# Windowed attention and a gated feed-forward layer: the second product of the last 3072 tokens as seven block products, stored transposed

## The chip, the cores and the metric

The kernel runs on one core of one Trainium2 chip, in one launch. The metric is the device time of that launch in microseconds. The core has five engines with queues of their own: TensorE (PE in the profile, its weight loads PEld), VectorE (DVE), ScalarE (ACT), GpSimd (POOL, here Pool) and SyncE (SP), which here issues every DMA. Each engine works through its instructions in order and waits on semaphores for the others.

## The reference

Attention over a window (first four heads) or a dilated window (last four), then a feed-forward layer with a gate, all in float32:

```python
scores = scale * np.matmul(q, k.transpose(0, 1, 3, 2))      # 8 batches x 8 heads x 576 tokens x 64
scores = np.where(masks[None, :, :, :], scores, -1000000000.0)
scores = scores - np.max(scores, axis=-1, keepdims=True)
attn = np.exp(scores)
attn = attn / (np.sum(attn, axis=-1, keepdims=True) + 1e-09)
x = np.matmul(attn, v)                                      # as 4608 tokens x 512
...
h = x @ w_in                                                # 512 x 2048
relu6 = np.clip(h + 3.0, 0.0, 6.0)
g = h * relu6 / 6.0
return g @ w_out                                            # 2048 x 512
```

## The kernel before

Every float32 product is made of three matmuls: each operand is split into a high half, rounded to fp32r, and the low half that is left, and high x high, high x low and low x high are added up in PSUM. A high half is a copy with a cast, a low half a subtraction.

The 4608 tokens are twelve chunks of 384 (CH). The first four (PLAIN) go through both products in the plain way: `gemm1` gives 128 features of a chunk, `relu`, `gate`, `gate_high` and `gate_low` make the gated halves, `gemm2` multiplies them with 128 rows of `w_out` into four 128x512 banks of PSUM. The features are 16 steps (NF) of 128.

The last eight chunks, 3072 tokens, are four groups of two chunks. Their **first product** is done in blocks of 2 x 2 (features in two halves, tokens in two halves, the inner dimension in two halves) with seven block products (A11, A12, S2, S1, S3, A22, S4) in place of eight; the sums of weight blocks that this needs are made once (`combo_words`, `combo_sum`, `combo_high`, `combo_low`), written to the DRAM tile `sums`, and read back in each group through a ring of eight SBUF slots (`load_sums`, 512 KB each, two products). The sums of tokens are made in `add_tokens` and split in `fill_high` and `fill_low`. For each of eight pairs of feature steps, `pair` issues the seven products (six matmuls of 384 columns each, L656 to L658) into banks x, y, z of PSUM. Between two products into the same bank ScalarE copies it out (`keep`, L911) and VectorE adds two banks (`add`, L917). Each pair gives four gated tiles of 128x384, which are split at once (L871 high on ScalarE, L875 low on VectorE).

Their **second product** is plain before the change: `unit_part` (L646 to L648) multiplies a gated tile's 128 tokens (as the stationary operand) with 128 rows of `w_out` (512 columns, moving), three matmuls each, into six banks of a group. These units stand on TensorE between the block products of `pair`, and fill the time in which a bank is read. `put_out` scales by 1/6 and writes 128 rows of the output.

Attention is done in 48 blocks of three (head, part) pairs (`block`). The first 12 are in the list ORDER, written by hand. The rest, `attend`, stand at places of the table SPOTS beside the plain chunks, two at once, and then one in each pair. A block's mask is added by VectorE (`add_mask`), then come `largest`, `shifted`, `exponent`; `normalise` divides by the sums.

What sets the order: TensorE's instructions stand in the order of the code. Those of the other engines are put in order by a planner (`_in_time`), from the durations and dependencies that each `op(...)` names; `ahead` says how early an operation may stand before its due time, `takes` and `gives` count slots of the pools `work` (16 tiles) and `wpool` (36) and of PSUM (`ps_h` two banks, `ps_a` six).

Of the kernel before, what the change touches and what calls it, by code (L numbers as in the profile page):

```python
# [39 lines left out]
SPOTS = (30, 1), (33, 1), (36, 1), (39, 1), (42, 1), (45, 1), (52, 1), (56, 1), (59, 1)  # L40
# [34 lines left out]
def windowed_attention_ffn(ctx: ExitStack, tc: tile.TileContext, qk, vp, w, mask, out):  # L75
# [24 lines left out]
    NT, DM = out.shape  # L100
# [147 lines left out]

    def exponent(t):
        return nc.scalar.activation(es[t], es[t], AF.Exp, scale=SCALE)  # L250

# [19 lines left out]
    def block(ts, tv, pools=()):  # L271
# [4 lines left out]
        masked = ts is not None and ts < NFIRST  # L276
# [222 lines left out]
    def gate_high(n):  # L499
        ghs[n] = work_tile("gh", F32R)  # L500
        return nc.scalar.copy(ghs[n], ts[n])
# [49 lines left out]
    STREAMED = (A11, A12, A22, S2, S4, S3, S1)  # L551
    GROUPS = (NCH - PLAIN) // 2
    STREAM = NF // 2 * PRODUCTS // 2
    sums = tc.dram_tile([2 * STREAM, P, 2, HALF], F32, name="sums")
    combos = {}

    def combo_words(k, i):

        if k not in combos:
            combos[k] = w_tile("v", [4, HALF])  # L560
        x, v = win[2 * k + i], combos[k]
        nc.vector.tensor_tensor(
            out=v[:, 2 * i : 2 * i + 2].rearrange("p a n -> p (a n)"), in0=x[:, 0].bitcast(F32), in1=x[:, 1].bitcast(F32), op=ALU.add
        )

    def combo_sum(k, i):

        v = combos[k]
        to, a, b, op = ((3, 2, 3, ALU.add), (2, 0, 2, ALU.subtract), (0, 3, 0, ALU.subtract), (1, 1, 0, ALU.subtract))[i]
        nc.vector.tensor_tensor(out=v[:, to], in0=v[:, a], in1=v[:, b], op=op)  # L570

    def combo_high(k):
        hi = w_tile("sh", [4, HALF], F32R)
        nc.scalar.copy(hi, combos[k])
        combos[k] = combos[k], hi

    def combo_low(k):
        v, hi = combos[k]
        nc.vector.tensor_tensor(out=v.bitcast(F32R), in0=v, in1=hi.bitcast(F32), op=ALU.subtract)

    def streamed(k, i):
        return PRODUCTS * k + STREAMED.index(i)

    def combo_plain(k):
        for i, x, at in ((A11, win[2 * k], 0), (A12, win[2 * k], HALF), (A22, win[2 * k + 1], HALF)):
            nc.sync.dma_start(out=sums[streamed(k, i)], in_=x[:, :, at : at + HALF].bitcast(F32))

    def combo_out(k):
        v, hi = combos.pop(k)
        at = streamed(k, S2)  # L590
        to = sums[at : at + 4].rearrange("n p a x -> p n a x")
        nc.sync.dma_start(out=to[:, :, 0], in_=hi.bitcast(F32))
        nc.sync.dma_start(out=to[:, :, 1], in_=v)
# [3 lines left out]
    def load_sums(at):  # L597
        ring[at] = w_tile("ring", [2, 2, HALF], F32R)
        i = 2 * (at % STREAM)
        nc.sync.dma_start(out=ring[at].bitcast(F32).rearrange("p n a x -> p n (a x)"), in_=sums[i : i + 2].rearrange("n p a x -> p n (a x)"))  # L600
# [35 lines left out]
    banks, begun, ended = {}, set(), {}  # L636

    def unit_part(g, f, at, gh, gl):
        if (g, at) not in banks:
            banks[g, at] = ps_a.tile([P, DM], F32, name="ps_o", tag="ps_a")  # L640
        bank, first = banks[g, at], (g, at) not in begun
        begun.add((g, at))
        ended[g, at] = ended.get((g, at), 0) + 1
        final = ended[g, at] == NF
        rows = slice(at % TT * P, (at % TT + 1) * P)
        nc.tensor.matmul(bank, lhsT=gh[:, rows], rhs=wt(f, 2), start=first, stop=False)  # L646
        nc.tensor.matmul(bank, lhsT=gh[:, rows], rhs=wt(f, 3), start=False, stop=False)  # L647
        nc.tensor.matmul(bank, lhsT=gl[:, rows], rhs=wt(f, 2), start=False, stop=final)  # L648

    def multiply(g, k, i, bank, start):  # L650

        at = streamed(k, i)
        tile_, (h, l) = ring[g * STREAM + at // 2][:, at % 2], cell(i)
# [39 lines left out]

    def op(engine, us, do, after=(), lag=0.0, takes=(), gives=(), before=(), ahead=AHEAD):
        plan.append(Operation(engine, us, do, [x for x in after if x is not None], lag, [(*x, 0)[:3] for x in takes], list(gives), list(before), ahead))
        return len(plan) - 1
# [6 lines left out]
    def turn_over(t, src, into, name, after):  # L703
        two = []

        def do():
            two.extend(turn_by_blocks(src.pop(t), name))
            into[t] = two[0]

        x = op("DVE", 0.92, do, [after], takes=TWO, gives=ONE, ahead=EVER)  # L710
        return [
            op("ACT", 0.6, lambda i=i: cross(*two, i), [x], gives=ONE if i else (), ahead=EVER) for i in range(2)
        ]

    def attend(bs, pools):
# [12 lines left out]
        for x in names.values():  # L728
            room[x] = room.get(x, 0) + 1
        beat = op(  # L730
            "PE", 0.35 + 0.535 * len(order), do,
# [4 lines left out]
        for ts in scores:  # L736
            x = op("DVE", 0.55, lambda ts=ts: add_mask(ts), [beat], takes=ONE, gives=[(names[ts], 1)], ahead=EVER)
            released[names[ts]].append(x)
            x = op("DVE", 0.55, lambda ts=ts: largest(ts), [x], ahead=EVER)
            x = op("DVE", 0.57, lambda ts=ts: shifted(ts), [x], ahead=EVER)  # L740
            x = op("ACT", 0.53, lambda ts=ts: exponent(ts), [x], ahead=EVER)
# [3 lines left out]
        for tv in values:  # L745
            x = op("DVE", 0.9, lambda tv=tv: normalise(tv), [beat], takes=ONE, gives=[(names[tv], 1)], ahead=EVER)
# [35 lines left out]

    def first(n, after):
        c, f = steps[n]
        g = op("PE", 12 * 0.173, lambda: gemm1(n), [*after, *released["ps_h"][-2:-1]], takes=[("ps_h", 1)], gives=SLOT if c == PLAIN - 1 else ())
# [3 lines left out]
        gh = op("ACT", 0.52, lambda: gate_high(n), [t], takes=ONE)  # L789
        gates[n] = gh, op("DVE", 0.58, lambda: gate_low(n), [gh], takes=ONE, gives=ONE)  # L790
        return g

    def second(n):
        c, f = steps[n]
        new = f == 0 and c >= 2
        x = op("PE", 9 * 0.227, lambda: gemm2(n), [*gates.get(n, ()), *(freed.pop(0) for _ in range(TT if new else 0) if freed)], takes=[("ps_a", TT)] if new else (), gives=TWO)
# [4 lines left out]
    def combine(k, before):  # L801
        x = op("DVE", 0.69, lambda: combo_words(k, 0), takes=[("w", 2, 1)], before=before)
        x = op("DVE", 0.69, lambda: combo_words(k, 1), [x])
        for i in range(4):
            x = op("DVE", 0.42, lambda i=i: combo_sum(k, i), [x])
        x = op("ACT", 1.05, lambda: combo_high(k), [x])
        x = op("DVE", 1.3, lambda: combo_low(k), [x])
        x = op("SP", 0.9, lambda: combo_out(k), [x], lag=3.5, gives=[("w", 2)], before=before)
        return x, op("SP", 1.35, lambda: combo_plain(k), lag=3.5, before=before)

    combined, ring_landed, ring_used = {}, {}, {}

    def bring(at):
        if at < GROUPS * STREAM:
            pairs = {(2 * (at % STREAM) + i) // PRODUCTS for i in range(2)}
# [381 lines left out]
```

## Time and profile before

| | |
|---|---|
| median of three timed runs | 862.8 us (862.38 to 863.41) |
| the profiled execution, its own time | 864.73 us |
| its span, first to last instruction | 863.0 us |
| granted TensorE clock, mean | 0.988 |
| group 0 to group 3, about | 347 to 860 us |

The profile tells of one execution. Its span is 1.7 us shorter than the time measured for that execution, which is 1.9 us above the median of the timed runs. In the views, a group of instructions has one line: line number, engine, operation, tiles (out<-in), sizes and count, then busy time and the mean duration of one in ns, then how long the engine stood idle before them and what ended that. In a timeline the columns are start, duration, and the instruction; in the table of windows, for each stretch, its length and the busy time of each engine.

### The profile page before, as it was taken

How to read it: one execution, taken by the hardware profiler on the slowest of the kernel's cores; microseconds unless marked ns; L12 is line 12 of the kernel's file. 1: busy time of each engine (PE TensorE's matmuls, PEld its weight loads, DVE VectorE, ACT ScalarE, POOL GpSimd, SP SyncE). 2: the span in 40 equal slices, each digit the busy share in tenths (PEclk: the TensorE clock that was granted, in tenths of full speed). 3: DMA queues.
4: the chain of work that ended last, by engine and by line, in shares of the span. 5: the costliest groups of instructions: out<-in, count | busy, mean ns of one | idle time of the engine just before them, and what ended most of it. 6: DMA issues, size and time to landing. Idle time of an engine off the chain costs nothing.

```text
span 863.0 us, 20520 instructions
## 1 busy us (share of the span) xinstructions
PE 848.5 (98%) x8540; PEld 756.6 (88%) x8540; DVE 563.0 (65%) x1148; ACT 496.3 (58%) x1034; POOL 31.3 (4%) x78
## 2 busy tenths in 40 slices
PE   7799999999999999999999999999999999999998
PEld 5588999899899999898898888888888889999997
DVE  4799996668887887655667665567566466343332
ACT  3688775357766657665556646545754545543334
POOL 0000000001201000100000000000000000000000
PEclk7799999999999999999999999999999999999999
DMA  8747433565583583654444646443735422853001
GB/s 285 267 147 240 123 117 118 179 205 183 184 256 130 189 286 112 243 171 159 137 137 150 246 153 208 138 136 122 273 113 152 155 80 92 301 177 107 1 1 73
DMA packets 69420, 141.18 MB, mean 164 GB/s; under 512 B 5200, under 2 KB 19536, under 8 KB 69328
## 3 DMA queue, kind: packets, MB, share of 16 engines
q1 hardware_dynamic: 69328, 139.88, 48.2%
q8 instruction: 67, 1.10, 0.5%
q14 instruction: 25, 0.20, 0.1%
HBM read 115.74 MB, written 24.12 MB: 162 GB/s over the span
## 4 chain that ended last, share of the span: by engine, by line
PE 96%; DVE 2%; issue 1%; ACT 0%; DMA 0%; SPq 0%
PE ps_o L646 11%; PE ps_o L648 10%; PE ps_o L647 10%; PE ps_x L656 9%; PE ps_x L658 9%; PE ps_x L657 9%; PE ps_h L486 5%; PE ps_h L487 5%; PE ps_h L488 5%; PE ps_o L536 5%; PE ps_o L538 5%; PE ps_o L537 5%; PE ps_b L221 2%; PE ps_a L203 1%; PE ps_a L221 1%; PE ps_b L203 1%
## 5 line engine op out<-in xcount | busy, mean ns | idle before, releaser
L646 PE MATMUL ps_o<-wo,gh 128*128 128x512 f32 x384 | 151.9, 396 | 0.0
L648 PE MATMUL ps_o<-wo,gl 128*128 128x512 f32 x384 | 150.2, 391 | 0.0
L647 PE MATMUL ps_o<-wo,gh 128*128 128x512 f32 x384 | 150.1, 391 | 0.0
L656 PE MATMUL ps_x<-xh,ring 128*128 128x384 f32 x384 | 129.5, 337 | 0.0
L657 PE MATMUL ps_x<-xl,ring 128*128 128x384 f32 x384 | 129.0, 336 | 0.0
L658 PE MATMUL ps_x<-xh,ring 128*128 128x384 f32 x384 | 129.0, 336 | 0.0
L911 ACT COPY s<-ps_x 128x384 f32<-128x384 f32 x96 | 45.8, 477 | 135.2 <-PE ps_x L658 132.4
L917 DVE TENSOR_TENSOR s<-ps_x,s 128x384 f32<-128x384 f32 x96 | 53.2, 555 | 100.9 <-ACT s L911 54.0
L875 DVE TENSOR_TENSOR gl<-t,gh 128x384 fp32r<-128x384 f32 x128 | 71.2, 557 | 54.4 <-ACT gh L871 51.8
L871 ACT CAST gh<-t 128x384 fp32r<-128x384 f32 x128 | 65.6, 514 | 47.5 <-DVE t L879 46.8
L486 PE MATMUL ps_h<-xh,wi 128*128 128x384 f32 x256 | 88.4, 345 | 0.0
L487 PE MATMUL ps_h<-xl,wi 128*128 128x384 f32 x256 | 86.4, 338 | 0.0
L488 PE MATMUL ps_h<-xh,wi 128*128 128x384 f32 x256 | 86.4, 338 | 0.0
L648 PEld LDWEIGHTS ps_o<-wo,gl 128*128 128x128 f32 x384 | 72.1, 188 | 15.6
L646 PEld LDWEIGHTS ps_o<-wo,gh 128*128 128x128 f32 x384 | 72.1, 188 | 11.7
L647 PEld LDWEIGHTS ps_o<-wo,gh 128*128 128x128 f32 x384 | 72.1, 188 | 10.0
L879 DVE SCALAR_TENSOR_TENSOR t<-t,s 128x384 f32<-128x384 f32 x96 | 53.9, 562 | 40.5 <-ACT t L867 39.0
L867 ACT ACTIVATE t<-s,three 128x384 f32<-128x384 f32 x96 | 59.2, 617 | 28.8 <-DVE s L917 28.0
L656 PEld LDWEIGHTS ps_x<-xh,ring 128*128 128x128 f32 x384 | 72.2, 188 | 3.9
L657 PEld LDWEIGHTS ps_x<-xl,ring 128*128 128x128 f32 x384 | 72.2, 188 | 3.9
L536 PE MATMUL ps_o<-wo,gh 128*128 128x512 f32 x192 | 74.9, 390 | 0.0
L538 PE MATMUL ps_o<-wo,gl 128*128 128x512 f32 x192 | 74.7, 389 | 0.0
(98 smaller groups left out, 1569.1 us busy)
## 6 DMA issues: line engine op xcount, KB each, us to landing
ring<-sums SPq DMA_DIRECT2D x112, 512.0 KB, 6.0
st<-in_w SPq DMA_DIRECT2D x32, 512.0 KB, 4.0
kq<-in_qk SPq DMA_DIRECT2D x39, 416.0 KB, 4.2
v<-in_v SPq DMA_DIRECT2D x39, 390.0 KB, 5.3
out<-o SPq DMA_DIRECT2D x36, 256.0 KB, 2.2
sums<-wi SPq DMA_DIRECT2D x24, 256.0 KB, 7.2
sums<-sh SPq DMA_DIRECT2D x8, 512.0 KB, 3.3
sums<-v SPq DMA_DIRECT2D x8, 512.0 KB, 4.1
```

The costliest lines, as they stand in the source:

```text
L486: nc.tensor.matmul(ph, lhsT=wt(f, 0)[:, ks], rhs=a, start=(kt == 0), stop=False)
L487: nc.tensor.matmul(ph, lhsT=wt(f, 0)[:, ks], rhs=b, start=False, stop=False)
L488: ins = nc.tensor.matmul(ph, lhsT=wt(f, 1)[:, ks], rhs=a, start=False, stop=(kt == NK - 1))
L536: nc.tensor.matmul(po[c][tt], lhsT=gh[:, rows], rhs=wt(f, 2), start=first, stop=False)
L538: return nc.tensor.matmul(po[c][tt], lhsT=gl[:, rows], rhs=wt(f, 2), start=False, stop=(f == NF - 1))
L646: nc.tensor.matmul(bank, lhsT=gh[:, rows], rhs=wt(f, 2), start=first, stop=False)
L647: nc.tensor.matmul(bank, lhsT=gh[:, rows], rhs=wt(f, 3), start=False, stop=False)
L648: nc.tensor.matmul(bank, lhsT=gl[:, rows], rhs=wt(f, 2), start=False, stop=final)
L656: nc.tensor.matmul(bank, lhsT=tile_[:, 0, ks], rhs=h[:, kt], start=(start and kt == 0), stop=False, skip_group_check=True)
L657: nc.tensor.matmul(bank, lhsT=tile_[:, 0, ks], rhs=l[:, kt], start=False, stop=False, skip_group_check=True)
L658: nc.tensor.matmul(bank, lhsT=tile_[:, 1, ks], rhs=h[:, kt], start=False, stop=(kt == 1), skip_group_check=True)
L875: nc.vector.tensor_tensor(out=two[1], in0=t[0], in1=two[0].bitcast(F32), op=ALU.subtract)
```

## The change

The second product of the four groups is done in blocks as well, transposed: for each group `out^T = w_out^T g` with `w_out`'s features in two halves, its 512 columns in two halves and the group's tokens in two halves. `w_out`'s blocks and their sums are the stationary operand and come from a second DRAM tile, `rights`, through the same ring; the gated tiles, and sums of them, are the moving one. The seven products of a group run one after the other over all eight pairs (RIGHT_TURNS), so the group's 32 gated tiles are kept in SBUF until then, unsplit. Each of the 56 steps of a group splits its moving tile when it is due: the high half on Pool, the low half on VectorE. The output of these tokens is stored by columns, and turned on the host.

In the first product, A11's result is copied from bank x into bank y, and A12 is added to it in PSUM by TensorE, in place of the add on VectorE. The order of the products is a new table (TURNS), in which A22 and S4 of a pair stand among the next pair's. No parts of the second product stand between them any more, but for the last three steps of a group.

Further: the masks of the 24 blocks after the first 12 are added by a matmul into the bank (MASKED); the exponents of the last 36 blocks take the negative maximum as their bias, six instructions of 64 columns on ScalarE, with no subtraction on VectorE; 16 blocks are normalised on ScalarE, six instructions each (SHARED); 36 of the plain chunks' high halves are made by Pool; SPOTS has eight places, and 22 attention blocks stand beside the groups' first products (BESIDE_FIRST).

```diff
-SPOTS = (30, 1), (33, 1), (36, 1), (39, 1), (42, 1), (45, 1), (52, 1), (56, 1), (59, 1)
+SPOTS = (35, 1), (38, 1), (41, 1), (44, 1), (47, 1), (50, 1), (53, 1), (56, 1)
+LEAD_SUMS = 300.0
+GAPS = {(0, 0): 2}
+LATER = 3
+MASKED = 24
+SHARED = 16
+WIPED = {(0, 0), (0, 1)}
+BESIDE_FIRST = {(g, k) for g in range(3) for k in range(8 if not g else 7)}
+HIGH_BY = ("pppppppp",) * 7
...
+    def scaled_largest(t):
...
+        nc.vector.tensor_reduce(out=mx, in_=ps[:, :CH].rearrange("p (s x) -> p s x", x=2 * QB), axis=AX.X, op=ALU.max)
+        nc.vector.tensor_scalar_mul(mx, mx, -SCALE)
+
+    def exponents(t, j):
...
+        for i in (2 * j, 2 * j + 1):
+            cols = slice(2 * QB * i, 2 * QB * (i + 1))
+            nc.scalar.activation(es[t][:, cols], ps[:, cols], AF.Exp, bias=mx[:, i : i + 1], scale=SCALE)
...
-        masked = ts is not None and ts < NFIRST
+        masked = ts is not None and ts < NFIRST + MASKED
...
+    rights = tc.dram_tile([PRODUCTS * NF // 2, P, 2, HALF], F32, name="rights")
+    PAIRS = NF // 2
+    TURNS = []
+    for k in range(PAIRS + 1):
+        now = [(k, A11), (k - 1, A22), (k - 1, S4), (k, S2), (k, A12), (k, S1), (k, S3)]
+        TURNS += [x for x in now if 0 <= x[0] < PAIRS]
...
+    RIGHT_TURNS = [
+        (p, k) for p, a, b in
+        ((R11, 0, 8), (T1, 0, 2), (R21, 0, 8), (T1, 2, 8), (T2, 0, 8), (R22, 0, 4), (T3, 0, 8), (R22, 4, 8), (T4, 0, 8))
+        for k in range(a * PAIRS // 8, b * PAIRS // 8)
+    ]
...
-        nc.tensor.matmul(bank, lhsT=gh[:, rows], rhs=wt(f, 2), start=first, stop=False)
-        nc.tensor.matmul(bank, lhsT=gh[:, rows], rhs=wt(f, 3), start=False, stop=False)
-        nc.tensor.matmul(bank, lhsT=gl[:, rows], rhs=wt(f, 2), start=False, stop=final)
...
+    def multiply_right(at, k, banks, two, start, parts):
+
+        right, (hi, lo) = ring[at][:, k % 2], two
+        for part in parts:
+            cols = slice(part * P, (part + 1) * P)
+            for i, (a, x) in enumerate(((0, hi), (0, lo), (1, hi))):
+                nc.tensor.matmul(
+                    banks[part][:, :CH], lhsT=right[:, a, cols], rhs=x, start=(start and not i), stop=(i == 2), skip_group_check=True
+                )
...
-        gh = op("ACT", 0.52, lambda: gate_high(n), [t], takes=ONE)
+        gh = op("POOL", 0.55, lambda: gate_high(n, nc.gpsimd.tensor_copy), [t], takes=ONE)
...
+            if (g, k) in WIPED:
+                def do():
+                    take()
+                    nc.tensor.matmul(at_bank["y"][:, :CH], lhsT=ident_b, rhs=mask_sb[:, 0], start=True, stop=True)
...
+            def copy():
+                if wipe is None:
+                    take()
+                nc.scalar.copy(at_bank["y"][:, :CH], at_bank["x"][:, :CH])
...
+            seeded = seed(first_product(g, k, A11, at_bank, "x"))
+            yield
+            s2 = keep("s2", first_product(g, k, S2, at_bank, "x", [seeded]))
+            yield
+            p2 = first_product(g, k, A12, at_bank, "y", [seeded])
+            gated(lambda: at_bank["y"][:, :CH], p2, g, 0, k, True)
+            yield
+            p5 = first_product(g, k, S1, at_bank, "z")
+            yield
+            s3 = keep("s3", first_product(g, k, S3, at_bank, "x", [s2]))
+            c22 = add("s3", "z", [s3, p5], ())
+            gated(lambda: kept["s3"], c22, g, 3, k, False)
+            yield
+            p4 = first_product(g, k, A22, at_bank, "x", [s3])
+            gated(lambda: at_bank["x"][:, :CH], p4, g, 1, k, True)
+            yield
+            p3 = first_product(g, k, S4, at_bank, "z", [c22])
+            c12 = add("s2", "z", [s2, p3], FREE)
+            gated(lambda: kept["s2"], c12, g, 2, k, False)
+            yield
...
+        def sum_of(name, to, x, y, alu, after, kk):
+
+            def do():
+                at = [gated_tiles[g, q, kk] for q in (to, x, y)]
+                nc.vector.tensor_tensor(out=at[0], in0=at[1], in1=at[2], op=alu)
...
+        def halves(p, k):
+
+            _, q, name = RIGHT_STEPS[p]
+            two, gives, after = [], [], [sums_of[name, k] if name else kept_gates[g, q, k], beats[-5]]
...
+            def high_():
+                two.append(work_tile("gh", F32R))
+                if by_pool:
+                    nc.gpsimd.tensor_copy(out=two[0], in_=gated_tile(g, q, k))
+                else:
+                    nc.scalar.copy(two[0], gated_tile(g, q, k))
+
+            def low_():
+                two.append(work_tile("gl", F32R))
+                nc.vector.tensor_tensor(out=two[1], in0=gated_tile(g, q, k), in1=two[0].bitcast(F32), op=ALU.subtract)
+
+            by_pool = HIGH_BY[p][k] == "p"
+            x = op("POOL" if by_pool else "ACT", 0.55, high_, after, takes=[("work", 1, 5)], ahead=8.0)
+            y = op("DVE", 0.58, low_, [x], takes=ONE, gives=gives)
```

**VectorE, inside a group.** Before, in the middle of a group, gates (`t<-t,s`, or from a bank `ps_x`), low halves (`gl`) and bank adds (`s`) of a pair alternate with an attention block's instructions (`e` scores, `z`, `x` shares, `mx` maxima):

```order
744 L879 SCALAR_TENSOR_TENSOR t<-t,s 128x384
745 L875 TENSOR_TENSOR gl<-t,gh 128x384
746 L879 SCALAR_TENSOR_TENSOR t<-t,ps_x 128x384
747 L917 TENSOR_TENSOR s<-ps_x,s 128x384
748 L875 TENSOR_TENSOR gl<-t,gh 128x384
749 L879 SCALAR_TENSOR_TENSOR t<-t,s 128x384
750 L875 TENSOR_TENSOR gl<-t,gh 128x384
751 L229 TENSOR_TENSOR e<-ps_b,mi 128x384
```

After, at the beginning of the second product of group 1, low halves of kept gated tiles (`gl<-g,gh`) alternate with sums of gated tiles over two pairs (`g<-g`, 768 columns); the last gates of the group's first product stand among them:

```order
818 L1144 TENSOR_TENSOR g<-g 128x768
819 L1179 TENSOR_TENSOR gl<-g,gh 128x384 x2
820 L987 SCALAR_TENSOR_TENSOR g<-t,s 128x384
821 L1179 TENSOR_TENSOR gl<-g,gh 128x384
822 L1144 TENSOR_TENSOR g<-g 128x768
823 L1179 TENSOR_TENSOR gl<-g,gh 128x384 x3
824 L1144 TENSOR_TENSOR g<-g 128x768
825 L1179 TENSOR_TENSOR gl<-g,gh 128x384 x2
826 L987 SCALAR_TENSOR_TENSOR g<-t,s 128x384
```

The halvings have moved from the first product, where each followed its gate, to the second, 56 in a group where there were 32, and 16 sums a group are new.

**TensorE, in the same groups.** Before, units of the second product (`ps_o<-wo`, 512 columns) stand between block products (`ps_x<-xh,ring`), here a few of each:

```order
3681 L646 MATMUL ps_o<-wo,gh 128x512
3682 L647 MATMUL ps_o<-wo,gh 128x512
3683 L648 MATMUL ps_o<-wo,gl 128x512
3684 L656 MATMUL ps_x<-xh,ring 128x384
3685 L657 MATMUL ps_x<-xl,ring 128x384
3686 L658 MATMUL ps_x<-xh,ring 128x384
```

After, where group 0 passes from the first product to the second, the last block product of a pair (S3, whose halves are `x7h` and `x7l`) is followed by the first step of the second product, all of 384 columns:

```order
3277 L732 MATMUL ps_x<-x7h,ring 128x384
3278 L733 MATMUL ps_x<-x7l,ring 128x384
3279 L734 MATMUL ps_x<-x7h,ring 128x384
3280 L723 MATMUL ps_o<-gh,ring 128x384
3281 L723 MATMUL ps_o<-gl,ring 128x384
3282 L723 MATMUL ps_o<-gh,ring 128x384 x2
3283 L723 MATMUL ps_o<-gl,ring 128x384
```

The second product has left the gaps of the first and follows it as a run of 336 matmuls a group, with the first products' last and the next group's first ones at its ends.

More of the change, by code (lines that the diff above doesn't have):

```diff
@@ L577, in combo_low, with combo_sum @@
[L577 to L593, printed above, removed]
+    def combo_sum(side, k, i, eng):
+        v = combos[side, k]
+        to, a, b, op = SUMS[side][i]
+        eng.tensor_tensor(out=v[:, to], in0=v[:, a], in1=v[:, b], op=op)
@@ L711, in turn_over @@
         return [
-            op("ACT", 0.6, lambda i=i: cross(*two, i), [x], gives=ONE if i else (), ahead=EVER) for i in range(2)
+            op("ACT", 0.7, lambda i=i: cross(*two, i), [x], gives=ONE if i else (), ahead=EVER) for i in range(2)
         ]
```

492 lines of the change are left out of this document (349 added, 143 removed).

## The prediction

> **What bounds the kernel now.** I read the page first, then the waits of TensorE alone, then the table of windows.
>
> ```profile
> span 863.0 us, 20520 instructions
> PE 848.5 (98%) x8540; PEld 756.6 (88%) x8540; DVE 563.0 (65%) x1148; ACT 496.3 (58%) x1034; POOL 31.3 (4%) x78
> ...
> PEclk7799999999999999999999999999999999999999
> ...
> PE 96%; DVE 2%; issue 1%; ACT 0%; DMA 0%; SPq 0%
> ```
>
> TensorE is busy for 848.5 of 863.0 us at a full granted clock after the first two slices, and the chain that ended last is 96% TensorE. A busy share alone would not settle it, since a matmul's busy time overlaps the next one's; its waits do.
>
> ```profile
> PE ps_a L203 <- issue: 3.4, 2, 3.1
> PE ps_a L296 <- ACT e L250: 2.6, 2, 1.9
> PE ps_a L296 <- DVE x L258: 2.1, 3, 1.0
> ```
>
> These are the three largest of six rows, and all belong to the attention of the first stage. The windows say the same, and show how full VectorE may be without TensorE noticing:
>
> ```profile
> core 0: us, PE busy (x) PEld busy (x) DVE busy (x) ACT busy (x) POOL busy (x), PEclk, DMA share, GB/s
> 60.00:80.00 20.00, 20.00 (x154) 18.58 (x153) 19.34 (x40) 15.96 (x32) 0.00 (x0) 1.00 0.75 231
> 120.00:140.00 20.00, 20.00 (x106) 18.59 (x105) 19.24 (x37) 14.65 (x27) 0.00 (x0) 1.00 0.26 82
> 347.00:464.00 117.00, 117.00 (x1125) 104.41 (x1124) 73.82 (x149) 68.21 (x147) 7.05 (x21) 1.00 0.48 164
> ```
>
> From 60 us on TensorE never stands still. In most of group 0 (347 to 464) VectorE is 63% and ScalarE 58% busy. So the time follows TensorE's issue time, until another engine falls behind it.
>
> **The change, part by part. TensorE.** A matmul's price here is the distance between starts, not its duration.
>
> ```profile
> 790.06 0.39 PE L646 MATMUL ps_o<-wo,gh 128*128 128x512 f32 x1
> ...
> 792.78 0.34 PE L656 MATMUL ps_x<-xh,ring 128*128 128x384 f32 x1
> ...
> 794.86 0.39 PE L646 MATMUL ps_o<-wo,gh 128*128 128x512 f32 x1
> ```
>
> Twelve matmuls of 512 columns start between 790.06 and 792.78: 0.2267 us each. Twelve of 384 columns follow up to 794.86: 0.1733 us each. The old second product of the last four groups is three groups of lines (L646 to L648) with 384 matmuls each, 1152 x 0.2267 = 261.1 us. The new one is, per group, seven products x 8 pairs x 6 matmuls of 384 columns: 4 x 336 = 1344, x 0.1733 = 232.9 us. That is **-28.2 us**, and nothing lies beside it, since TensorE is the chain.
>
> Twenty-four score blocks now get their mask as a matmul, and two banks are wiped by one.
>
> ```profile
> 54.21 0.33 PE L279 MATMUL ps_a<-mi 32*128 32x384 bf16 x1
> 54.47 0.24 PE L213 MATMUL ps_a<-v,a 64*32 64x65 f32 x1
> ```
>
> Such a mask occupies TensorE for 54.47 - 54.21 = 0.26 us; 26 x 0.26 = **+6.8 us**. The number of attention blocks, transposes and first products is the same. TensorE's own work is thus 21.4 us shorter.
>
> **VectorE in the second product.** Here the cover has to be worked out, because the order of the changed kernel puts 56 halvings (L1179) and 16 sums (L1144) into the 56 steps of each group's second product.
>
> ```profile
> L875 DVE TENSOR_TENSOR gl<-t,gh 128x384 fp32r<-128x384 f32 x128 | 71.2, 557 | 54.4 <-ACT gh L871 51.8
> L879 DVE SCALAR_TENSOR_TENSOR t<-t,s 128x384 f32<-128x384 f32 x96 | 53.9, 562 | 40.5 <-ACT t L867 39.0
> L634 DVE TENSOR_TENSOR xl<-t,xh 128x768 fp32r<-128x768 f32 x12 | 11.2, 954 | 0.6 <-ACT xh L630 0.4
> L627 DVE TENSOR_TENSOR t<-raw,t 128x768 f32<-128x768 f32 x8 | 7.6, 950 | 0.0
> ```
>
> From a group's first halving to the first gate of the next group VectorE has 56 x 0.557 = 31.2 (halvings), 16 x 0.95 = 15.2 (sums, priced as the sums of tokens, L627), 4 x 0.56 = 2.2 (outputs added), 4 x 0.95 + 7 x 0.954 = 10.5 (the next group's input sums and halves), 7 x 0.56 = 3.9 (last gates and adds) and, in groups 0 and 1, some 2.3 for one attention block: 65.3, 65.3, 63.0, and 52.5 us in the last group, which fills nothing. TensorE has beside it 56 x 6 x 0.1733 = 58.2 plus eight first products of 1.04 = 8.3, and in groups 0 and 1 one attention block. What one costs:
>
> ```profile
> 478.76 0.39 PE L648 MATMUL ps_o<-wo,gl 128*128 128x512 f32 x1
> ...
> 480.18 0.50 PE L646 MATMUL ps_o<-wo,gh 128*128 128x512 f32 x1
> ```
>
> 480.18 - 478.76 less one slot of 0.23 is 1.2 us. So TensorE takes 67.7, 67.7, 66.5, and 63.4 us (five first products) in the last group. The cover holds, at 96% in the first two groups: slack 2.4, 2.4, 3.5 and 10.9 us. VectorE ran at 96 to 97% between 60 and 80 and between 120 and 140 us with no wait of TensorE, so I charge nothing for that alone.
>
> **Pool beside VectorE.** All 224 high halves of the second product move to Pool. A copy of 128x384 takes 0.51 us there, half a step of 1.04. Pool's rows have no cast to fp32r of this size; the other end is its subtraction into fp32r:
>
> ```profile
> L393 POOL TENSOR_TENSOR xl<-xf,xh 128x384 fp32r<-128x384 f32 x2 | 2.3, 1155 | 201.1 <-PE ps_b L203 200.4 <-ACT xh L387 0.7
> ```
>
> At 1.155 Pool would set the step, and 224 x 0.115 = 26 us would be lost. A cast reads one tile as a copy does, so I take 0.51 and charge nothing. But the two engines meet:
>
> ```profile
> 296.67 0.42 DVE L570 TENSOR_TENSOR v<-v 128x256 f32<-128x256 f32 x1
> 296.71 0.75 POOL L395 COPY raw<-xf 128x384 f32<-128x384 f32 x1 [29.39 <-ACT xf L334]
> ```
> ```profile
> 341.48 0.51 POOL L395 COPY raw<-xf 128x384 f32<-128x384 f32 x1 [40.46 <-ACT xf L334]
> ```
> ```profile
> 352.84 0.95 POOL L395 COPY raw<-xf 128x96 f32<-128x96 f32 x3 [1.58 <-ACT xf L334]
> 353.45 0.65 DVE L879 SCALAR_TENSOR_TENSOR t<-t,s 128x384 f32<-128x384 f32 x1 [0.53 <-ACT t L867]
> ```
> ```profile
> L879 DVE SCALAR_TENSOR_TENSOR t<-t,s x96: 516/558/655, 335.8 to 852.3; 128x384 f32<-128x384 f32 x96
> ```
>
> A copy that started under a VectorE sum of two SBUF tiles took 0.75 instead of 0.51 us, 0.24 more. A gate that started inside a run of Pool's copies took 0.65 where the median is 0.558; the longest of 96 took 0.655. So one meeting has cost VectorE up to 0.10 us here, and Pool 0.24. For VectorE's loss per Pool copy, c, the ends are 0 and 0.24 (what a full exchange of roles would give); I take 0.06, near VectorE's own rows but under their worst, since not every copy meets the reading part of a VectorE instruction. Per group 56 x 0.06 = 3.4, over the slack by 1.0, 1.0, 0 and 0: **+2.0 us**.
>
> The Trainium skill, "SBUF — State Buffer", section "Who interferes with whom", speaks against this change: a VectorE instruction with two SBUF inputs and a GpSimd instruction that reads SBUF exclude each other, and the later one blocks fully until the first is done. The copy that took 0.75 us agrees with it; the gate that took 0.65 agrees only if a copy holds the port for a small part of its time. By the rule at its harshest the sum would be that of the second rival below.
>
> **ScalarE and the banks in the first product.** The old code put parts of the second product between a block product and the next one into the same bank; now other block products stand there. A22 follows S3 into bank x with one product between them, once ScalarE has copied it.
>
> ```profile
> 784.35 0.34 PE L658 MATMUL ps_x<-x7h,ring 128*128 128x384 f32 x1
> ...
> 784.73 0.48 ACT L911 COPY s<-ps_x 128x384 f32<-128x384 f32 x1 [2.57 <-PE ps_x L658]
> ```
>
> The copy ends 784.73 + 0.48 - 784.35 = 0.86 us after the last matmul's start, 0.69 after its slot; 1.04 lies between, so 0.35 is free, unless ScalarE is in another instruction (L867, the longest, 0.62, below): a wait of up to 0.27. An attention block stands in this place in 19 of 32 pairs, and two steps of the second product in four; the other nine cost 0 to 2.4 us. I take **+1.5**.
>
> **What hides the rest.** The second weight's sums cost VectorE what the first's do now:
>
> ```profile
> L570 DVE TENSOR_TENSOR v<-v 128x256 f32<-128x256 f32 x32 | 14.4, 453 | 0.3
> L562 DVE TENSOR_TENSOR v<-wi 128x512 f32<-128x512 f32 x16 | 10.6, 685 | 0.0
> L579 DVE TENSOR_TENSOR v<-v,sh 128x1024 fp32r<-128x1024 f32 x8 | 9.8, 1224 | 2.6 <-ACT sh L574 2.4
> ```
> ```profile
> 140.00:340.00 200.00, 200.00 (x2545) 180.64 (x2544) 155.41 (x334) 121.17 (x265) 12.81 (x24) 1.00 0.58 191
> ```
>
> That is 14.4 + 10.6 + 9.8 = 34.8 us, most of it before group 0, where VectorE has 200 - 155.4 = 44.6 us free even without the maskings and shares that leave it. The exponents and shares that move to ScalarE are weighed as the first rival. The ring now brings 56 pieces per group where it brought 28:
>
> ```profile
> ring<-sums SPq DMA_DIRECT2D x112, 512.0 KB, 6.0
> ```
> ```profile
> 750.00:755.00 5.00, 5.00 (x26) 4.50 (x26) 1.47 (x3) 1.54 (x4) 0.00 (x0) 1.00 1.05 392
> ```
>
> A piece feeds two products, 2.08 us; at 392 GB/s its 524 kB take 1.34. With an attention block's 0.83 MB (2.1 us) a pair needs 3.5 x 1.34 + 2.1 = 6.8 of its 8.5 us. Eight slots cover 16.6 us against a landing of 6.0. I charge nothing; were only four slots ahead, 8.3 us, pieces queued behind an attention block's loads would be late by parts of a microsecond.
>
> The end: the last copy and a transfer of 384 instead of 256 KB, within 0.5 us of before. **Sum:** -28.2 + 6.8 + 2.0 + 1.5 = -17.9 us. The profiled execution took 864.7 us (863.0 of span, 1.7 around it), 1.9 above the median of 862.8; taken off the median, **844.9**.
>
> **The rivals.** *ScalarE sets the pace of the first product.*
>
> ```profile
> L334 ACT COPY a<-a_t 32x192 f32<-32x192 f32 x144 | 50.4, 350 | 6.4 <-DVE a L327 2.1 <-DVE z L255 1.6
> L867 ACT ACTIVATE t<-s,three 128x384 f32<-128x384 f32 x96 | 59.2, 617 | 28.8 <-DVE s L917 28.0
> L250 ACT ACTIVATE e<-e 128x384 f32<-128x384 f32 x48 | 24.9, 524 | 11.7 <-DVE e L244 11.1
> ```
>
> Between 192 columns (0.350) and 384 (0.524) a column costs 0.9 ns, so an exponent of 64 columns some 0.23. A pair with an attention block then has 4 x 0.6 + 3 x 0.48 + 8 x 0.35 + 6 x 0.23 = 8.0 us of ScalarE beside 7 x 1.04 + 1.2 = 8.5 of TensorE, 94%. For it: TensorE waits directly for the three copies of each pair. Against it: the attention block itself widens the narrowest window by 1.2. Twenty-two pairs x three copies x 0.2 us of lateness = 13: 858.
>
> *Pool and VectorE exclude each other at full price, slower than before.* With c = 0.24, 13.4 us per group, the excess is 11.0 + 11.0 + 9.9 + 2.5 = 34.4 instead of 2.0, the time 877. It turns the sign from c = 0.17 (168 x 0.17 less the slack of 8.3 eats the 19.9 left). For it is the 0.24 of Pool's copy, against it that VectorE's own rows show 0.10 at worst.
>
> *The narrower matmul does not keep its spacing,* so that the change does not save what it counts. A weight load lasts 0.188 us in the trace, longer than 0.1733; were it the spacing, 1344 x 0.0147 = 19.8 us return and take the other waits' place: 862.8 - 21.4 + 19.8 = 861. Against it: the twelve rows above have loads of the same size and keep 0.1733.
>
> *All waits stay hidden:* 862.8 - 21.4 = 841.4.
>
> **How the numbers follow.** The forecast (842.5 to 852) has 0.55, everything hidden 0.15, ScalarE 0.13, Pool 0.12, the spacing 0.05. The low end is the hidden case with a mask at the 0.1733 of any 384 columns, 26 x 0.087 = 2.3 less, 839; I write 838. Upward the range takes in ScalarE and the spacing, to 861. Outside stay Pool's case and a little more. A measurement of this kernel can tell 0.2%, 1.7 us. Faster: 0.55 + 0.15 + 0.13 = 0.83; the same 0.05; slower 0.12.
>
> **What would show it.** In the profile after: 384-column starts 0.173 apart in the second product, some 21 us less TensorE time; waits of TensorE from 340 us on of 3 to 8 us in all, on gl (VectorE) in the second product and on s or ps_x (ScalarE) in the first. Halvings over 0.70 us on average with Pool copies over 0.75 would show the exclusion at full price; waits for ring would show the transfers; ScalarE's copies starting late would show the first rival. What would make it wrong most is a chain over Pool, VectorE and TensorE that never gets ahead, since a step has only 1.04 us.

## The result, and the profile after

The changed kernel takes **868.4 us** (median of four runs, 866.8 to 869.1) where the kernel before takes 862.9 on the same chip: a ratio of 1.0061, 95% interval 1.0044 to 1.0078. It is slower by 0.6%. The forecast was 844.9, in a range of 838 to 861: wrong in sign, and outside the range.

The page of the changed kernel, the lines that answer to those shown of before, with VectorE's, Pool's and the transfers' rows over the 40 slices beside them:

```profile
span 865.0 us, 22224 instructions
PE 837.4 (97%) x8758; PEld 774.1 (89%) x8758; DVE 699.1 (81%) x1307; ACT 477.8 (55%) x1170; POOL 225.6 (26%) x338
...
DVE  4899986567767988966999977999876899545995
...
POOL 0000000010132220000858001558001458001574
PEclk8999999999999999998999999999999999999999
DMA  8856435235338799999974998974988773996371
...
PE 78%; DVE 10%; issue 5%; DMA 4%; ACT 2%; POOL 1%; SPq 0%; DVEq 0%; POOLq 0%
```

TensorE is no longer alone on the chain that ended last: 78% where it was 96%, and VectorE has 10%, the transfers 4%. VectorE's busy time has gone from 563 to 699 us. Two places stand out: where Pool works (four humps, the second products), VectorE is full; and before the first hump the transfers are at nine tenths or more for several slices. The groups of instructions name the first:

```profile
L1173 POOL CAST gh<-g 128x384 fp32r<-128x384 f32 x224 | 170.5, 793 | 131.8 <-DVE g L987 61.4
L723 PE MATMUL ps_o<-gl,ring 128*128 128x384 f32 x448 | 154.2, 344 | 5.8 <-DVE gl L1179 4.7
L1179 DVE TENSOR_TENSOR gl<-g,gh 128x384 fp32r<-128x384 f32 x224 | 152.5, 719 | 1.0 <-POOL gh L1173 1.0
...
L1144 DVE TENSOR_TENSOR g<-g 128x768 f32<-128x768 f32 x64 | 75.2, 1175 | 0.0
```

A halving takes 719 ns where its like took 557, a sum of gated tiles 1175 where the sum of tokens took 950, and Pool's cast 793 where a copy of the size took 510. The waits of TensorE name the second:

```profile
PEld ps_o L723 <- DVE gl L1179: 17.1, 36, 0.8
...
PE ps_b L231 <- DMA v<-in_v: 5.0, 3, 3.4
...
PE ps_o L723 <- DVE gl L1179: 4.7, 13, 0.5
...
PE ps_a L339 <- ACT e L277: 3.6, 3, 1.9
...
PE ps_x L732 <- DMA ring<-sums: 2.7, 3, 1.5
```

(In all, number of waits, the longest.) The matmuls themselves wait for VectorE's low halves for 4.7 us only, but their weight loads (PEld) for 17.1, and for two kinds of transfers the matmuls wait 7.7. Sums of waits of two queues that overlap are hard to add, so the lengths of the phases tell more. The windows of the changed kernel are, in turn, first and second product of groups 0 to 3:

```profile
core 0: us, PE busy (x) PEld busy (x) DVE busy (x) ACT busy (x) POOL busy (x), PEclk, DMA share, GB/s
331.00:415.00 84.00, 76.24 (x1122) 69.91 (x1121) 65.12 (x149) 62.80 (x166) 5.84 (x13) 0.96 1.06 387
415.00:487.00 72.00, 69.02 (x461) 63.24 (x460) 70.46 (x100) 22.30 (x51) 48.20 (x66) 1.00 0.72 250
487.00:549.00 62.00, 62.00 (x888) 59.92 (x887) 48.21 (x113) 54.79 (x146) 8.23 (x19) 1.00 0.95 335
549.00:617.00 68.00, 66.74 (x461) 63.54 (x460) 67.90 (x96) 14.38 (x26) 41.18 (x50) 1.00 0.72 242
617.00:678.00 61.00, 61.00 (x789) 58.92 (x788) 43.79 (x103) 51.01 (x130) 8.54 (x20) 1.00 0.86 304
678.00:745.00 67.00, 65.62 (x365) 62.82 (x365) 66.63 (x90) 12.90 (x22) 37.96 (x49) 1.00 0.69 237
745.00:799.00 54.00, 54.00 (x312) 54.00 (x311) 24.93 (x47) 26.50 (x52) 3.79 (x7) 1.00 0.89 314
799.00:861.00 62.00, 61.70 (x349) 59.92 (x347) 56.21 (x78) 6.67 (x13) 37.09 (x49) 1.00 0.45 162
```

In the first product of group 0 the transfers run at 387 GB/s with a busy share above 1, TensorE is busy for 76 of 84 us, and its granted clock falls to 0.96. In the second products of groups 0 to 2 VectorE is busy for 67 to 70 of 67 to 72 us. The first products of groups 1 to 3 show TensorE without a gap.

### The profile page after: what moved, and what is told of

Same layout as the page of the kernel before. It is cut to its first block, busy times and chain, and to the rows that moved or that the text cites. A ratio compares the mean times of both kernels' runs of the same rounds, so it can differ in the third digit from the quotient of the medians.

```text
span 865.0 us, 22224 instructions
## 1 busy us (share of the span) xinstructions
PE 837.4 (97%) x8758; PEld 774.1 (89%) x8758; DVE 699.1 (81%) x1307; ACT 477.8 (55%) x1170; POOL 225.6 (26%) x338
## 4 chain that ended last, share of the span: by engine, by line
PE 78%; DVE 10%; issue 5%; DMA 4%; ACT 2%; POOL 1%; SPq 0%; DVEq 0%; POOLq 0%
PE ps_o L723 15%; PE ps_x L732 8%; PE ps_x L733 8%; PE ps_x L734 8%; DVE gl L1179 6%; PE ps_h L529 5%; PE ps_h L530 5%; PE ps_h L531 5%; PE ps_o L579 5%; PE ps_o L581 5%; PE ps_o L580 5%; DVE g L1144 2%; DMA v<-in_v 2%; PE ps_b L231 2%; PE ps_a L213 1%
## 5 line engine op out<-in xcount | busy, mean ns | idle before, releaser
L723 PE MATMUL ps_o<-gh,ring 128*128 128x384 f32 x896 | 231.9, 335 | 0.1
L1173 POOL CAST gh<-g 128x384 fp32r<-128x384 f32 x224 | 170.5, 793 | 131.8 <-DVE g L987 61.4
L723 PEld LDWEIGHTS ps_o<-gh,ring 128*128 128x128 f32 x896 | 162.4, 188 | 0.8 <-POOL gh L1173 0.4
L723 PE MATMUL ps_o<-gl,ring 128*128 128x384 f32 x448 | 154.2, 344 | 5.8 <-DVE gl L1179 4.7
L1179 DVE TENSOR_TENSOR gl<-g,gh 128x384 fp32r<-128x384 f32 x224 | 152.5, 719 | 1.0 <-POOL gh L1173 1.0
L723 PEld LDWEIGHTS ps_o<-gl,ring 128*128 128x128 f32 x448 | 84.0, 188 | 17.8 <-DVE gl L1179 17.1
L732 PEld LDWEIGHTS ps_x<-xh,ring 128*128 128x128 f32 x384 | 72.6, 189 | 5.9 <-DMA ring<-sums 2.9
L1144 DVE TENSOR_TENSOR g<-g 128x768 f32<-128x768 f32 x64 | 75.2, 1175 | 0.0
L579 PE MATMUL ps_o<-wo,gh 128*128 128x512 f32 x192 | 75.1, 391 | 0.0
L581 PE MATMUL ps_o<-wo,gl 128*128 128x512 f32 x192 | 74.7, 389 | 0.0
L580 PE MATMUL ps_o<-wo,gh 128*128 128x512 f32 x192 | 74.7, 389 | 0.0
L734 PEld LDWEIGHTS ps_x<-xh,ring 128*128 128x128 f32 x384 | 72.6, 189 | 0.0
```

Source lines behind the costliest of these rows:

```text
L579: nc.tensor.matmul(po[c][tt], lhsT=gh[:, rows], rhs=wt(f, 2), start=first, stop=False)
L580: nc.tensor.matmul(po[c][tt], lhsT=gh[:, rows], rhs=wt(f, 3), start=False, stop=False)
L581: return nc.tensor.matmul(po[c][tt], lhsT=gl[:, rows], rhs=wt(f, 2), start=False, stop=(f == NF - 1))
L723: nc.tensor.matmul(banks[part][:, :CH], lhsT=right[:, a, cols], rhs=x, start=(start and not i), stop=(i == 2), skip_group_check=True)
L732: nc.tensor.matmul(bank, lhsT=tile_[:, 0, ks], rhs=h[:, kt], start=(start and kt == 0), stop=False, skip_group_check=True)
L734: nc.tensor.matmul(bank, lhsT=tile_[:, 1, ks], rhs=h[:, kt], start=False, stop=(kt == 1), skip_group_check=True)
```

## The experiments

Two causes were put to the test: that Pool's casts and VectorE's instructions keep each other out in the second products, and that the transfers hold up the first product of group 0. Their rivals: a chain over three engines that is too tight whoever stands in it, and ScalarE with the banks.

**High halves on ScalarE (e1).**

```diff
-HIGH_BY = ("pppppppp",) * 7
+HIGH_BY = ("aaaaaaaa",) * 7
```

> All 224 high halves of the second product are made by ScalarE, none by Pool; nothing else is changed. Exclusion theory (Pool's casts and VectorE's two-input instructions keep each other out): the halvings gl<-g,gh fall from 719 to about 557 ns and the sums g<-g from 1175 to about 950 ns, VectorE is no longer at 20.0 of 20 us in the second products, these shrink from 72, 68, 67 and 62 us to about 64 each (62 in the last), and the time from 868 to about 852 us. Rival (the chain over three engines is too tight whoever makes the high half): the instructions get shorter, the phases stay within 2 us of what they are, time 865 to 870. In both, the first product of group 0 stays at 84 us.

Measured: 856.5 us against 864.3 of before, ratio 0.9919 (0.9899 to 0.9939); against the changed kernel's 1.0061 that is 1.4% or 12 us less. The groups of this run:

```profile
L1179 DVE TENSOR_TENSOR gl<-g,gh 128x384 fp32r<-128x384 f32 x224 | 116.4, 553 | 27.0 <-ACT gh L1175 25.3 <-PE ps_o L723 1.3 <-issue 0.3
L1175 ACT CAST gh<-g 128x384 fp32r<-128x384 f32 x224 | 104.3, 512 | 29.0 <-PE ps_o L723 20.6 <-DVE g L1144 7.6 <-DVE gl L1179 0.5
L1144 DVE TENSOR_TENSOR g<-g 128x768 f32<-128x768 f32 x64 | 60.7, 950 | 0.0
```

The durations are back at 553 and 950 ns, and VectorE now idles before halvings, waiting for ScalarE. The second products take 67.1, 64.7, 63.3 and 60.2 us. The rival falls: a chain of three engines stays, with ScalarE in Pool's place, and TensorE's matmuls wait for it for 2.1 us in all. The time is 4 to 5 us above the 852 that were expected: the first of the four stretches is 3 us longer than expected, and group 0 begins 2.4 us later than in the changed kernel (333.5 against 331.1).

**The second weight's sums not written (e2).**

```diff
-        for to, x, at in pieces:
+        for to, x, at in pieces if not side else []:
...
-        for part, x in enumerate((hi.bitcast(F32), v)):
+        for part, x in enumerate((hi.bitcast(F32), v) if not side else ()):
...
-            rows = rights[first_row : first_row + 2]
+            rows = sums[first_row : first_row + 2]
```

> The second weight's blocks and their sums are made but not written to DRAM, and the second product reads the first weight's rows of the same size in their place (so the output of the last 3072 tokens is another); 40 transfers, 14.7 MB, are gone, and the order of everything else is kept. Transfer theory (group 0 begins with the transfers at their limit, 380 to 394 GB/s from 320 to 420 us): the first product of group 0 falls from 84 to about 73 us, TensorE's waits for v and ring vanish, the time falls by about 10, to 858. Rival (ScalarE and the banks set that phase): 84 us stay, time 866 to 869. The second products stay as they are in both.

Measured: 858.5 us, ratio 0.9943 (0.9924 to 0.9962), 1.2% or 10 us under the changed kernel. The two windows are the first and the second product of group 0:

```profile
332.00:406.00 74.00, 74.00 (x1124) 68.72 (x1123) 65.42 (x150) 62.94 (x167) 5.84 (x13) 1.00 0.83 284
406.00:478.00 72.00, 69.06 (x460) 63.26 (x459) 70.47 (x99) 22.25 (x51) 48.25 (x66) 1.00 0.69 233
```

The first product has shrunk from 84 to 74 us, with TensorE busy throughout at full clock; VectorE's and ScalarE's work in it is the same (65 and 63 us), so they were not what held it. In the changed kernel 387 GB/s x 84 us = 32.5 MB had to pass in this phase, here 284 x 74 = 21.0: the 11.5 MB between are nearly all writes of `rights`, of which 25 of the 40 (10.0 MB) are issued in this phase and more are under way at its start. At the 390 GB/s that stand there, 32.5 MB need 83 us. The second products are unchanged, as both theories had it.

**Both (e3).** The edits of e1 and e2 together.

> Both of the other two edits at once: high halves on ScalarE, second weight's sums not written (same change of the output). If the two causes are apart and complete, the time is that of TensorE's own work, some 21 us under the kernel before: 842 +- 3. If a third cause is there (ScalarE in the first products, the narrower matmul), it stays at 850 or more.

Measured: 845.5 us, ratio 0.9784 (0.9763 to 0.9806). That is half a microsecond above what was expected, on a chip where before ran at 864.3. The interval puts it 16.7 to 20.5 us under before; TensorE's own work is 21.4 less. The two causes explain the loss to within a few microseconds; no third of their size is left.

**Plain blocks written early, high halves on ScalarE (e4).** This is the whole computation.

```diff
+            op("SP", 1.35, lambda: combo_plain(side, k), [words[side, k]], lag=3.5, ahead=EVER),
...
-            combined[side, k].append(
-                op(
-                    "SP", 1.35, lambda: combo_plain(side, k), [words[side, k], taken[side, f - 1], x],
-                    lag=3.5, gives=[("w", 2)], ahead=EVER,
-                )
-            )
+            plan[x].after.append(combined[side, k][1])
+            plan[x].gives.append(("w", 2))
```

> The whole computation: high halves on ScalarE, and the plain blocks of both weights (48 transfers of 256 KB) are written as soon as their sums are formed in the order, not when the weight is last used. Transfer theory: part of the 12.6 MB moves ahead of 300 us, the first product of group 0 falls from 84 to 75 to 81 us, time 843 to 850. Rival (the transfers only move within the same stretch, since sums of the second weight stand late in the order): 84 us stay and the time is that of the first run of these.

Measured: **843.7 us**, ratio 0.9769 (0.9752 to 0.9786): 2.3% faster than the kernel before, 2.9% than the changed one. The page and the windows of group 0:

```profile
PE 92%; DMA 2%; DVE 2%; ACT 1%; issue 1%; SPq 0%; DVEq 0%
```
```profile
332.00:408.00 76.00, 74.33 (x1123) 68.56 (x1122) 64.20 (x150) 65.54 (x170) 4.76 (x13) 1.00 1.04 381
408.00:474.00 66.00, 65.58 (x463) 64.66 (x464) 58.22 (x99) 45.40 (x105) 5.91 (x12) 1.00 0.78 277
```

The first product of group 0 takes 76 us. It moves 381 x 76 = 29.0 MB, 3.5 less than the changed kernel; the stretch from 140 us to it ran at 219 GB/s where it ran at 202, which over 191 us is the 3.2 MB that went ahead. The transfers are still at their limit in this phase, and TensorE almost without waits.

**Pool writes, but reads nothing (e5).**

```diff
-                    nc.gpsimd.tensor_copy(out=two[0], in_=gated_tile(g, q, k))
+                    nc.gpsimd.memset(two[0].bitcast(F32), 1.0)
```

> As the changed kernel, but each of Pool's 224 instructions of the second product fills the high half's tile with a constant in place of copying the gated tile into it (so the second product is of other numbers): Pool is as far in the chain of three engines as before, and reads no SBUF. Exclusion by reading (two-input VectorE instructions and Pool's reads): halvings back to about 557 ns and sums to about 950, second products as with ScalarE (67, 65, 63, 60 us), time 868 less 11 to 13 = about 856. If any Pool instruction beside VectorE does it, or the hand-over from Pool to VectorE as such: 700 ns and 868 us stay.

The halves are then 1 and g - 1, which still add up to g, so the second product is not of other numbers, as the expectation had it, only split in another way. Measured: 851.0 us, ratio 0.9868 (0.9852 to 0.9885), 1.9% or 17 us under the changed kernel, more than the 11 to 13 that were expected; the durations are as expected.

```profile
L1179 DVE TENSOR_TENSOR gl<-g,gh 128x384 fp32r<-128x384 f32 x224 | 118.1, 553 | 15.1 <-PE ps_o L723 9.7 <-POOL gh L1173 3.8 <-issue 1.4
L1173 POOL MEMSET gh<- 128x384 f32 x224 | 91.1, 421 | 194.3 <-PE ps_o L723 114.6 <-DVE g L987 65.0 <-DVE gl L1179 10.3
L1144 DVE TENSOR_TENSOR g<-g 128x768 f32<-128x768 f32 x64 | 60.8, 951 | 0.0
```

With 224 Pool instructions beside it that write the same tiles, VectorE keeps its 553 and 951 ns. For halvings and sums, what costs is Pool's reading, not its presence or its hand-over. That it matters how many SBUF tiles VectorE reads is seen in the changed kernel itself, in two forms of the same gate (count, then shortest, median and longest in ns):

```profile
L987 DVE SCALAR_TENSOR_TENSOR g<-t,ps_x x64: 514/553/556, 338.9 to 804.1; 128x384 f32<-128x384 f32 x64
L987 DVE SCALAR_TENSOR_TENSOR g<-t,s x64: 514/557/852, 370.3 to 818.3; 128x384 f32<-128x384 f32 x64
```

The gate that reads a bank and one SBUF tile never took over 0.556 us, the one that reads two SBUF tiles up to 0.852. Of the gates, bank adds and outputs that read a bank and one SBUF tile, 28 overlapped one of these Pool casts, and none of them took over 0.558.

**Early writes, high halves on Pool (e6).** The edit of e4 without that of e1.

> The whole computation: the plain blocks written early as in e4, high halves on Pool as in the changed kernel. If the two causes add up, 868 less the 13 that early writing took off the run with ScalarE: 855 to 857, with the first product of group 0 at about 76 us and the second products still at 72, 68, 67 and 62. If early writing only helped because ScalarE made the halves: 866 or more.

Measured: 858.7 us, ratio 0.9954 (0.9939 to 0.9970), a little above what was expected; first product of group 0 at 74.4, second products at 72.5, 68.6, 67.2 and 61.9. With the changed kernel, e1 and e4 this makes a square of four: early writing is worth 1.1% with Pool and 1.5% with ScalarE, ScalarE 1.4% and 1.9%. The causes add up, roughly.

**Masks by VectorE (e7).** MASKED = 0 on top of e4.

> The whole computation, e4 with the 24 masks again added by VectorE (no mask matmul in the planned blocks). By the price of the mask term (24 x 0.26 us) TensorE's work falls by 6.3 us; if VectorE, with some 13 us more in the plain chunks and group 0, still keeps up: 837 to 839 us. Rival (VectorE or the order of transfers falls behind in group 0 and the 6.3 us come back as waits): 843 or more.

Measured: 843.8 us, ratio 0.9772 (0.9749 to 0.9796): the same as e4. The phases show where the 6.3 us went: the plain chunks and the first product of group 0 end 4.4 us earlier than in e4, the second product of group 0 takes 70.4 us in place of 65.6. Its waits of TensorE:

```profile
PE ps_o L723 <- ACT gh L1174: 2.1, 3, 0.8
...
PE ps_x L732 <- DMA ring<-sums: 1.0, 1, 1.0
```

So what the missing mask matmuls gave back, 4.4 us at most, was lost again at once. That is what one would see if the matmuls buy time of VectorE that is needed, but which instruction is late at that place was not tried. Nor does this run measure a mask's price: 2.0 of the 4.4 us had been gained when the phase began, and that start differs by more between runs with the same code up to there (331.1 us in the changed kernel, 333.5 in e1, 330.1 in e5).

**Plain chunks' high halves on ScalarE (e8).** On top of e4, all 64 on ScalarE.

> The whole computation, e4 with the 36 high halves of the plain chunks on ScalarE again, so that Pool makes none at all. TensorE waited for nothing in the plain chunks, so the exclusion there should have cost nothing: 842 to 846, the same as e4. If those Pool casts delayed the sums of weights and so the transfers of group 0: 841 or less.

Measured: 850.5 us, ratio 0.9860 (0.9843 to 0.9876): slower than e4 by 0.9%. The plain chunks end 1.6 us later, which is within the spread of that start, but the two products of group 0 take 78.8 and 67.6 us in place of 75.7 and 65.6.

```profile
PE ps_b L231 <- DMA v<-in_v: 3.5, 1, 3.5
```

The longest wait is again for an attention block's load behind the ring. Both expectations fell: taking Pool's casts away there gains nothing, and the start of group 0 gets worse. ScalarE is fuller there and the order of all engines is another; which of the two does it was not settled.

The phases of all runs side by side, in us, from the starts of their first matmuls in the timelines:

| | first product, group 0 | second product, groups 0, 1, 2, 3 | ratio to before |
|---|---|---|---|
| changed kernel | 84.0 | 72.4, 68.4, 67.2, 61.9 | 1.0061 |
| e1 high halves on ScalarE | 84.9 | 67.1, 64.7, 63.3, 60.2 | 0.9919 |
| e2 `rights` not written | 73.6 | 72.4, 68.4, 67.2, 61.9 | 0.9943 |
| e3 both | 74.3 | 68.7, 64.7, 63.3, 60.2 | 0.9784 |
| e4 early and ScalarE | 75.7 | 65.6, 64.7, 63.3, 60.2 | 0.9769 |
| e5 Pool does not read | 84.3 | 65.9, 64.7, 63.3, 60.2 | 0.9868 |
| e6 early and Pool | 74.4 | 72.5, 68.6, 67.2, 61.9 | 0.9954 |

The first products of groups 1 to 3 take 61.3, 60.9 and 53.5 us in every one of them, to 0.1 or 0.2.

## Why the prediction was wrong, step by step

**TensorE's own work, -28.2 and +6.8: right.** In the last group of e4 the second product, 336 matmuls and two block products (348 in all), takes 60.2 us, which is 0.173 each; the spacing held in a long run, and the third rival falls. A mask's matmul was followed by the next one after 0.26 us in 28 of the 36 places that now have one. With both causes of loss reduced, e4 is 19.9 us under before by its ratio, where 21.4 were counted.

**Pool beside VectorE, "I take 0.06": mis-sized by a factor of four.** VectorE lost 224 x (719 - 553) + 64 x (1175 - 950) ns = 51.6 us, 0.23 per Pool cast. That this is the upper end of the range, 0.24, is in part chance, since it is an average over two kinds: 125 of the 224 halvings took 0.85 us, 0.30 more than alone, and 94 took 0.55. The mistake was in the choice of the row. The gate that took 0.65 met copies of 96 and 192 columns; the row with the whole 384 columns was the other, the copy that was held for 0.24, and it was priced as Pool's loss alone. That VectorE's own rows showed "0.10 at worst" holds for the gates only. In the same trace of before, sums of two SBUF tiles met Pool's subtraction (the first line gives shortest, median and longest in ns):

```profile
L570 DVE TENSOR_TENSOR v<-v x32: 383/420/1110, 161.0 to 308.9; 128x256 f32<-128x256 f32 x32
205.85 1.29 POOL L393 TENSOR_TENSOR xl<-xf,xh 128x384 fp32r<-128x384 f32 x1 [200.43 <-PE ps_b L203]
206.31 1.11 DVE L570 TENSOR_TENSOR v<-v 128x256 f32<-128x256 f32 x1
```

The sum that started inside the subtraction took 1.11 us instead of 0.42, a loss of 0.69, and ended at 207.42, 0.28 after Pool did. The gate that took 0.65 ended 0.31 after the last of Pool's copies, one of 96 columns that lasts 0.36 us. Both fit a VectorE instruction that is held until Pool is done; the gate lost little because the copy in its way was short. The prediction's sentence on the Trainium skill ("SBUF — State Buffer", section "Who interferes with whom") weighed the rule and let that gate count against it, which these rows do not bear out. The runs agree with the rule where they test it: with casts that read, 719 ns (the changed kernel); with fills that only write, 553 (e5); with nobody, 553 (e1). The prediction's own mark for the full price, halvings over 0.70 us and Pool's copies over 0.75, is what the profile after shows.

In time this cost the second products 5.3 + 3.7 + 3.9 + 1.7 = 14.6 us (changed kernel against e1), 15.8 against e5, where +2.0 stood in the sum. The second rival, at full price, gave 34.4, because the cover was mis-sized as well: the sum left VectorE 2.4, 2.4, 3.5 and 10.9 us to spare, 19.2 in all. In e4, where Pool does not meet it, the window of group 0's second product (408 to 474 us) has 7.8 us without VectorE, and those of groups 1 to 3 are these:

```profile
535.00:600.00 65.00, 65.00 (x464) 64.66 (x464) 56.43 (x98) 38.34 (x82) 0.00 (x0) 1.00 0.75 257
661.00:724.00 63.00, 63.00 (x365) 63.00 (x364) 52.90 (x90) 35.56 (x76) 0.00 (x0) 1.00 0.74 252
777.00:838.00 61.00, 61.00 (x352) 60.72 (x351) 44.44 (x79) 30.31 (x66) 0.00 (x0) 1.00 0.45 165
```

That is 43 us to spare in all, of which 8 are left in the changed kernel: 35 of VectorE's 51.6 us went into idle time, and the rest made the stretches longer. (The prediction's stretches end a little later, so the two slacks compare only roughly.) The turning point, 0.17, falls with the slack: e2 has all of the exclusion and none of the transfers' loss, and is 0.6% faster than before.

**"I charge nothing" for the transfers: the step that failed outright.** The working took the ring's steady state, and there it was right: groups 1 to 3 run at 304 to 335 GB/s in their first products without a wait. It did not count what else passes in the first product of group 0: the second weight's sums and plain blocks. The prediction placed their VectorE work "most of it before group 0" and never placed their 14.7 MB. The queue of the changed kernel shows them among the ring's pieces there (start, duration of the issuing instruction, transfer):

```profile
353.01 2.39 SPq L650 DMA_DIRECT2D rights<-wo  x3
355.56 0.50 SPq L673 DMA_DIRECT2D ring<-sums  x1
356.25 1.03 SPq L659 DMA_DIRECT2D rights<-sh  x1
357.38 0.45 SPq L659 DMA_DIRECT2D rights<-v  x1
357.89 1.32 SPq L673 DMA_DIRECT2D ring<-sums  x1
```

The loss is 10 us (84.0 to 73.6, e2).

**ScalarE and the banks, +1.5, and the first rival, 858: nothing.** The groups of the changed kernel, with forms kept apart, have the exponents of 64 columns in these rows:

```profile
L274 ACT ACTIVATE e<-ps_b,mx 128x64 f32<-128x64 f32 x96 | 24.6, 318 | 13.4 <-DVE mx L266 7.3 <-DVE z L282 3.2 <-DVE z L298 2.9
...
L274 ACT ACTIVATE e<-e,mx 128x64 f32<-128x64 f32 x72 | 20.8, 339 | 1.1 <-DVE mx L266 0.8
...
L274 ACT ACTIVATE e<-ps_a,mx 128x64 f32<-128x64 f32 x48 | 13.0, 346 | 0.1
```

In the first products of groups 1 to 3 TensorE has no gap in any run. The rival's price of an exponent was too mild: one of 64 columns takes 0.32 to 0.35 us, not 0.23, and by its own count a pair would then have 8.6 us of ScalarE beside some 8.5 of TensorE. The window of group 1 shows less, 54.8 us of ScalarE in 62, or 88%; which part of the count was too high was not traced. The copies that TensorE waits for come in time.

**The sum.** -21.4 for TensorE, some +15 for the exclusion, +10 for the transfers make +4; measured were +5.5. The error lies in two terms outside TensorE: a meeting of two engines priced from a meeting with short copies, and transfers judged by their mean load in one steady stretch.

## What to carry to other kernels

When a matmul-bound kernel is given fewer matmuls, the time goes to whichever engine or queue fills first in each stretch, so add up the load of every engine and the bytes of the transfers stretch by stretch, the first one with its set-up work above all. Moving element-wise work to Pool is not free for a VectorE that is near full with two-input instructions on SBUF tiles: here it cost VectorE 0.23 us per cast of 128x384, and ScalarE, with room, did the same at no cost to VectorE. Between a range's ends, take the value of the row that has the same shape and the same role, not of the row on the engine one is pricing, and look at the longest duration of every group that reads the same way, not of one group alone.

## What the hardware showed beyond that

- Pool's cast of 128x384 from f32 to fp32r took 793 ns on average beside VectorE's two-input work, 502 to 512 in the 13 of 224 cases that no such work overlapped, 654 in the plain chunks, and its fill of the same tile 421.
- A small VectorE instruction with one SBUF input can be held as well, and by Pool's fills too. The scaling of the maxima, 6 columns, takes 0.172 us; in e5 one that started inside a run of Pool's copies and fills took 1.423 (1.106 in the changed kernel, beside copies and casts):

```profile
L266 DVE TENSOR_SCALAR mx<-mx x36: 171/172/1423, 193.6 to 638.7; 128x6 f32<-128x6 f32 x36
```

- Where TensorE starved, its granted clock was lower too: 0.86 between 380 and 400 us, where it was busy for 14.4 of 20 us beside transfers at 394 GB/s, and 1.00 in the same 20 us of e2, where it was busy throughout. What the clock alone cost was not separated.
- An instruction of 64 columns on ScalarE (0.32 to 0.35 us) cost two thirds of one of 384 (0.52): six of them for one tile are 2.0 us where one instruction was 0.52.
